# One DMA queue instead of two: bulk loads and gradient stores issued by GpSimd between the zero fill's pieces

## The chip, the cores and the metric

The kernel runs on one core of a Trainium2 chip. The metric is device time in microseconds of that core, the median over several runs. A core has five engines: TensorE (PE, with its weight loads as PEld), VectorE (DVE), ScalarE (ACT), GpSimd (POOL) and SyncE (SP). DMAs that any of them issues are carried out by the core's 16 DMA engines.

## What is computed

One decode step of a transformer block with its whole backward pass. The forward pass is a layer norm, attention of one query token over the last 4,096 positions of a key and value cache, and a gated feed-forward network, with residual sums:

```python
W = min(4096, max(256, Sk // 4))                 # Sk = 32768, so W = 4096
k = repeat(k_cache[:, :, Sk - W:, :], rep)       # B = 2, 8 KV heads, 32 query heads, Dh = 128
v = repeat(v_cache[:, :, Sk - W:, :], rep)
p = softmax(einsum("bhqd,bhkd->bhqk", q, k) * Dh ** -0.5)
h = x + (p @ v).reshape(B, 1, Hq * Dh) @ wo      # D = 512
h2 = h + (gelu(ln(h) @ w_gate) * (ln(h) @ w_up)) @ w_down   # F = 1792
out, vjp = jax.vjp(f, x, k_cache, v_cache, wq, wo, w_gate, w_up, w_down)
return out, *vjp(grad_out)
```

All is bf16. Nine outputs are written: the block's output and eight gradients. Two of them, those of the two caches, have the caches' full size, 2 x 8 x 32768 x 128. Only their last 4,096 positions are not zero, so most of what the kernel writes is zeros: 224 MiB of zeros, 32 MiB of cache gradients that aren't zero, and some 13 MiB of weight gradients.

## The kernel before

**The zero fill.** A tile `zt` of 128 x 2048 bytes is set to zero on POOL (L315). A DMA from it that casts bytes to float32 writes 1 MiB of zeros from all 128 partitions; this is called a column here. There are 32 regions (two caches, two batches, eight heads) of seven columns. `zero_cast(i)` (L110) writes region i with one DMA of seven columns, or, for regions 8, 16 and 24, with six or seven DMAs listed in `ZERO_PARTS` (L107), some of which have 15 rows or fewer, so that the 16 DMA engines do not all receive the same number of bytes. 29 regions are issued at once in `prefetch(0, 0)`; the last three are cut into pieces of one or two columns, and `zero_next` (L127) issues one piece after each store of a cache gradient.

**The stages.** In order: layer norm and query; `attention(0)`, the pass over batch 0's eight KV heads (called groups g); `middle(0)`, the feed-forward network forward and backward with the output projection; `score_grads(0)`, which reads batch 0's V tiles again; the same three for batch 1, the last one interleaved with the weight gradients (`add_group`, L713); the gradient of wq (L801 to L810); and at the end the cache gradients, 16 stores of 2 MiB from eight staging tiles (L823 to L847).

**Memory.** Almost all tiles are byte ranges of one buffer `mem`, at offsets written by hand. Batch 0's K tiles use four slots in turn, so the K of group g+3 can be loaded once group g-1 is done. Batch 0's V tiles have a slot for each group, which batch 1's V tiles take over when `score_grads(0)` has read them. Batch 1's K of groups 5 and 7 take the slot of batch 1's K 0; K 2, 3 and 4 take slots of batch 0's V 5, 6 and 7, and batch 1's V 5, 6 and 7 take them back. `wg` and `wu` share bytes with batch 0's K slots.

**The order of DMAs.** `prefetch(b, g)` (L306) is called at the start of each group and issues that moment's loads: K by `load_k` (L149), V by `load_v` (L153), `wo` (L323), `wg` (L167) and `wu` (L170), all on SP (`nc.sync`). The weight gradients are stored on SP as well (L737, L755, L762, L810). The zeros and the stores of cache gradients are on POOL (`nc.gpsimd`, L114, L130, L844). A scheduler orders PE, DVE and ACT, but SP and POOL are told to keep the order of the program:

```python
ctx.enter_context(tc.manual_schedule(engines={mybir.EngineType.SP, mybir.EngineType.Pool}))
```

So an instruction on SP or POOL that waits for a buffer holds back all that follow it on the same engine.

Of the kernel before, what the change touches and what calls it, by code (L numbers as in the profile page):

```python
# [8 lines left out]
F32 = mybir.dt.float32  # L9
U8 = mybir.dt.uint8  # L10
U32 = mybir.dt.uint32
ACT = mybir.ActivationFunctionType
ALU = mybir.AluOpType
# [3 lines left out]
P = 128  # L17
# [7 lines left out]
F = 1792  # L25
# [43 lines left out]
def kernel(ctx, tc, A_x, A_k_cache, A_v_cache, A_wq, A_wo, B_x, B_w_gate, B_w_up, B_w_down, grad_out,  # L69
# [36 lines left out]

    ZERO_PARTS = {8: ((4, 1), (15, 2), (2, 2), (15, 14), (12, 2), (P, 4), (16, 7)), 16: ((4, 1), (15, 2), (2, 2), (15, 14), (12, 2), (P, 4), (16, 7)), 24: ((3, 16), (15, 2), (3, 4), (15, 18), (12, 2), (P, 4))}  # L107
    ZERO_FIRST, ZERO_CUTS = 29, (1, 1, 1, 2, 2)

    def zero_cast(i):  # L110
        dst, done = zero_regions[i].bitcast(F32), 0
        for rows, n in ZERO_PARTS.get(i, ((P, ZPK // P),)):
            src = zt[0:rows * (P // rows):P // rows, :]
            nc.gpsimd.dma_start(out=dst[done * ZE:(done + rows * n) * ZE].rearrange("(p k e) -> p k e", p=rows, k=n),  # L114
                                in_=src.unsqueeze(1).to_broadcast([rows, n, ZE]))
            done += rows * n
        assert done == ZPK

    zero_pieces = []
    for i in range(ZERO_FIRST, len(zero_regions)):  # L120
        done = 0
        for k in ZERO_CUTS:
            zero_pieces.append(zero_regions[i].bitcast(F32)[done:done + P * k * ZE].rearrange("(p k e) -> p k e", p=P, k=k))
            done += P * k * ZE
        assert done == ZPK * ZE

    def zero_next():  # L127
        if zero_pieces:
            dst = zero_pieces.pop(0)
            nc.gpsimd.dma_start(out=dst, in_=zt[:].unsqueeze(1).to_broadcast([P, dst.shape[1], ZE]))  # L130

# [16 lines left out]

    def load_k(b, g):  # L149
        Kt[b, g] = at(K_OFF[b][g], [P, NJ, DH], BF16, f"K{b}_{g}")  # L150
        nc.sync.dma_start(out=Kt[b, g][:], in_=Kv[:, b, g, :, :])

    def load_v(b, g):  # L153
        Vt[b, g] = at(OFF_V + g * 8 * KIB, [P, NJ, DH], BF16, f"V{b}_{g}")
        nc.sync.dma_start(out=Vt[b, g][:], in_=Vv[:, b, g, :, :])

# [10 lines left out]
    def load_wg():  # L167
        nc.sync.dma_start(out=wg[:], in_=B_w_gate.rearrange("(p r) f -> p r f", r=NDR))

    def load_wu():  # L170
        nc.sync.dma_start(out=wu[:], in_=B_w_up.rearrange("(p r) f -> p r f", r=NDR))

# [133 lines left out]
    def prefetch(b, g):  # L306
        if b == 0:
            if g == 0:
                load_k(0, 0)
                load_wd(OFF_WD0)  # L310
                load_v(0, 0)
                for i in range(1, 4):
                    load_k(0, i)
                    load_v(0, i)
                nc.gpsimd.tensor_scalar(out=zt[:], in0=wq_sb[:, 0, 0:ZE // 2].bitcast(U8),  # L315
                                        scalar1=0, scalar2=None, op0=ALU.mult)
                for i in range(ZERO_FIRST):
                    zero_cast(i)
            elif g + 3 < HKV:
                load_k(0, g + 3)  # L320
                load_v(0, g + 3)
            elif g == 5:
                nc.sync.dma_start(out=wo_sb[:], in_=A_wo.rearrange("(p r) n -> p r n", r=NOR))  # L323
            elif g == 6:
                load_wg()
            elif g == HKV:
                load_wu()
                load_k(1, 0)
                load_k(1, 1)
        else:  # L330
            if g == 0:
                for i in range(5):
                    load_v(1, i)
                for i in range(2, 5):
                    load_k(1, i)
            elif g == 1:
                load_k(1, 5)
            elif g == 2:
                load_k(1, 6)
            elif g < 6:  # L340
                load_v(1, g + 2)
            elif g == 6:
                load_k(1, 7)
            elif g == HKV:
                load_rows(nc.sync)
                load_wd(OFF_WD)
# [351 lines left out]
    with tc.tile_pool(name="ps_G", bufs=2, space=PSUM) as ps_G:  # L698
# [35 lines left out]

        for (r0, nr) in ((0, 14), (14, 14), (28, 4)):
            add_group([D] * nr, lambda k, r0=r0: Ro_flat[:, (r0 + k)::NOR], lambda k: DH_bf[:],
                      lambda st, r0=r0, nr=nr: nc.sync.dma_start(out=gwo_v[:, r0:r0 + nr, :],  # L737
                                                                 in_=st[:, :nr * D].rearrange("p (a n) -> p a n", n=D)))
        row_box = {}

        def rows_from_T(key, srcT_bf):
# [3 lines left out]
            for r in range(NFR):  # L745
                if r == 8:
# [7 lines left out]
        add_group([D] * NFR, lambda k: row_box["act"][:, k::NFR], lambda k: dh2_bf,  # L754
                  lambda st: nc.sync.dma_start(out=gwd_v, in_=st[:, :NFR * D].rearrange("p (a n) -> p a n", n=D)))  # L755
        for (key, srcT, o_dram) in (("dg", dgT_bf, out_6), ("du", duT_bf, out_7)):
            grad_units.append(lambda key=key, srcT=srcT: rows_from_T(key, srcT))
            o_v = o_dram.rearrange("(p r) f -> p r f", r=NDR)
            pieces = [(r, f0, fl) for r in range(NDR) for (f0, fl) in ((0, 512), (512, 512), (1024, 512), (1536, 256))]
            add_group([fl for (_, _, fl) in pieces], lambda k, pieces=pieces: ln2_bf[:, pieces[k][0]::NDR],  # L760
                      lambda k, key=key, pieces=pieces: row_box[key][:, pieces[k][1]:pieces[k][1] + pieces[k][2]],
                      lambda st, o_v=o_v: nc.sync.dma_start(out=o_v, in_=st[:, :NDR * F].rearrange("p (r f) -> p r f", r=NDR)))  # L762
        g_next = [0]
# [9 lines left out]
    with tc.tile_pool(name="ps_W2", bufs=2, space=PSUM) as ps_W, \  # L773
# [27 lines left out]
        for r in range(NDR):  # L801
            st = at(OFF_WQ + r * 8 * KIB, [P, HQ * DH], BF16, "gq")
            for c4 in range(4):
                ps = ps_G.tile([P, 1024], F32, tag="ps_g", name="ps_gq")
                for q in range(2):
                    col0 = c4 * 1024 + q * 512
                    nc.tensor.matmul(out=ps[:, q * 512:(q + 1) * 512], lhsT=L_bf[:, r::NDR],  # L807
                                     rhs=Ro_flat[:, col0:col0 + 512], start=True, stop=True)
                evac(st[:, c4 * 1024:(c4 + 1) * 1024], ps[:])
            nc.sync.dma_start(out=gwq_v[:, r, :], in_=st[:])  # L810

    with tc.tile_pool(name="ps_G3", bufs=3, space=PSUM) as ps_G, \
# [4 lines left out]
        def bd_of(n):  # L817
# [3 lines left out]
            return build_bd(OFF_BD + n * 8 * KIB, rowsb[:], f"bd{n}")  # L821
        nxt = bd_of(0)
        for n, (b, what) in enumerate(jobs):  # L823
            rhs_bd = nxt
            lhs_bf, dst_v = (ds_bf[b], dKv) if what else (p_bf[b], dVv)
            for gq in range(2):
# [15 lines left out]
                for a in range(2):  # L842
                    g0 = gq * 4 + a * 2
                    nc.gpsimd.dma_start(out=dst_v[:, b, g0:g0 + 2, :, :], in_=sts[a][:])  # L844
                    zero_next()
                if gq == 0 and n + 1 < len(jobs):
# [28 lines left out]
```

## Time and profile before

| what | before |
|---|---|
| median of 6 runs | 791.89 us (791.62 to 792.25) |
| the profiled execution | 792.06 us |
| its span | 790.3 us |
| bytes moved by DMA | 332.44 MB, 421 GB/s over the span |
| HBM read, written | 49.30 MB, 282.33 MB |
| busy: PE, DVE, ACT, POOL | 559.3, 473.4, 281.2, 65.6 us |
| POOL's DMAs from `zt` | 61 |
| SP's loads of K and V | 32, of 1 MiB each |

The span runs from the first to the last instruction of the profiled execution; its time is 1.76 us longer. The page cuts the span into 40 slices of 19.76 us; each digit is a busy share in tenths. A queue's line gives packets, MB and the share of the span of 16 engines that its packets took, waiting included. Lines of stretches give start and end, length, the busy time and number of instructions of PE, PEld, DVE, ACT and POOL, then the granted clock of TensorE, the DMA share and GB/s. Lines of waits give who waited for whom, the time in total, how often, and the longest. Lines in order of time give start, duration, engine, line, operation and, in brackets, the idle time before and what ended it.

### The profile page before, as it was taken

To read this page: it belongs to the slowest core of one execution; us is meant where nothing else is said; L and a number is where in the kernel's file an instruction comes from. 1 tells how busy PE (TensorE), PEld (TensorE's weight loads), DVE (VectorE), ACT (ScalarE), POOL (GpSimd) and SP (SyncE) were. 2 spreads that over 40 slices of the span, in tenths; PEclk is the share of its full clock that TensorE was granted. 3 is DMA by queue.
4 is the path that set the end of the run, shared out by engine and by line. 5 is a ranking of instruction groups with operands and counts; after the bars stand their busy time and mean duration, and the time that the engine had idled before them with its cause. 6 is when DMAs were issued, how large, how long until landed. Compare 5 with 4: busy or idle time off the path is not lost. (4 is left out here: it accounts for less than half of the span.)

```text
span 790.3 us, 12404 instructions
## 1 busy us (share of the span) xinstructions
PE 559.3 (71%) x5032; PEld 303.4 (38%) x5096; DVE 473.4 (60%) x1161; ACT 281.2 (36%) x406; POOL 65.6 (8%) x97
## 2 busy tenths in 40 slices
PE   3899998587688988760647877978798766787000
PEld 3656564254566555420423453433233222222000
DVE  2599999126632989770551377675635799898000
ACT  1534330124345424100201352645444466587000
POOL 4300000000020000000030000000000012111100
PEclk9999999868698999895787776975568598799555
DMA  8999999999999999999999999999999999999997
GB/s 366 418 418 422 418 427 424 424 430 428 427 423 418 423 426 423 427 425 428 429 427 429 428 428 427 429 420 427 427 429 427 427 423 427 428 429 426 428 428 291
DMA packets 41418, 332.44 MB, mean 421 GB/s; under 512 B 2432, under 2 KB 2448, under 8 KB 2576
## 3 DMA queue, kind: packets, MB, share of 16 engines
q0 software_dynamic: 34416, 268.44, 88.5%
q1 hardware_dynamic: 6932, 63.19, 37.4%
q8 instruction: 40, 0.66, 0.3%
q10 hardware_dynamic: 12, 0.01, 0.2%
q14 instruction: 18, 0.15, 0.0%
HBM read 49.30 MB, written 282.33 MB: 420 GB/s over the span
## 5 line engine op out<-in xcount | busy, mean ns | idle before, releaser
L422 DVE TENSOR_TENSOR mem<-mem,ee 128x512 bf16<-128x512 bf16 x512 | 181.1, 422 | 42.0 <-PE KT_ps L378 30.6
L433 PE MATMUL M_ps<-mem 128*128 128x512 bf16 x468 | 135.2, 390 | 9.7 <-DVE mem L422 6.1
L836 PE MATMUL ps_g<-mem 128*128 128x512 bf16 x250 | 79.6, 414 | 26.4 <-DVE mem L91 23.8
L380 ACT COPY mem<-KT_ps 128x1024 bf16<-128x1024 bf16 x64 | 63.3, 1014 | 83.8 <-PE KT_ps L378 77.9
L91 DVE CAST mem<-ps_g 128x512 bf16<-128x512 f32 x128 | 82.6, 687 | 9.3 <-ACT mem L93 7.9
L93 ACT CAST mem<-ps_g 128x512 bf16<-128x512 f32 x128 | 74.5, 585 | 33.3 <-PE ps_g L836 26.0
L114 POOL DMA_DIRECT2D out_dram<-zt x46 | 37.0, 1080 | 502.3 <-DMA out_dram<-zt 502.0
L378 PE MATMUL KT_ps<-ident_bf,mem 128*128 128x128 bf16 x512 | 47.1, 237 | 33.7 <-DMA mem<-in_A_k_cache_dram 28.7
L254 PE MATMUL ps_tb<-ident_bf,mem 128*128 128x128 bf16 x480 | 55.8, 250 | 11.4 <-DMA mem<-in_B_w_gate_dram 4.7
L433 PEld LDWEIGHTS <-mem 128*128 128x128 bf16 x512 | 43.6, 99 | 49.1 <-issue 15.2
L836 PEld LDWEIGHTS <-mem 128*128 128x128 bf16 x256 | 26.3, 103 | 79.1 <-issue 66.4
L93 ACT COPY mem<-ps_tb 128x512 bf16<-128x512 bf16 x44 | 25.7, 585 | 74.6 <-PE ps_tb L254 69.8
L254 PEld LDWEIGHTS <-mem 128*128 128x128 bf16 x480 | 37.3, 128 | 36.5 <-issue 30.4
L378 PEld LDWEIGHTS <-mem 128*128 128x128 bf16 x512 | 35.4, 106 | 39.4 <-DMA mem<-in_A_k_cache_dram 29.2
L656 PE MATMUL VT_ps<-ident_bf,mem 128*128 128x128 bf16 x512 | 46.4, 238 | 3.2 <-ACT mem L93 1.1
L656 PEld LDWEIGHTS <-mem 128*128 128x128 bf16 x512 | 36.3, 107 | 27.7 <-issue 20.1
L665 PE MATMUL dP_ps<-mem 128*128 128x512 bf16 x114 | 40.4, 431 | 4.8 <-ACT mem L93 4.7
L93 ACT COPY mem<-VT_ps 128x1024 bf16<-128x1024 bf16 x31 | 31.7, 1022 | 33.5 <-PE VT_ps L656 32.3
L91 DVE COPY mem<-ps_tb 128x512 bf16<-128x512 bf16 x44 | 18.7, 424 | 41.2 <-PE ps_tb L254 39.9
L727 PE MATMUL ps_gr<-mem 2*128 2x512 bf16 (+1 forms) x78 | 33.8, 498 | 12.8 <-DVE mem L747 7.4
L91 DVE CAST mem<-ps_gr 128x512 bf16<-128x512 f32 (+1 forms) x38 | 24.7, 654 | 27.8 <-PE ps_gr L727 27.8
L91 DVE COPY mem<-VT_ps 128x1024 bf16<-128x1024 bf16 x33 | 23.1, 700 | 27.6 <-PE VT_ps L656 27.1
(244 smaller groups left out, 630.5 us busy)
## 6 DMA issues: line engine op xcount, KB each, us to landing
out_dram<-zt POOLq DMA_DIRECT2D x26, 7168.0 KB, 101.8
out_dram<-mem POOLq DMA_DIRECT2D x16, 2048.0 KB, 31.5
mem<-in_A_k_cache_dram SPq DMA_DIRECT2D x16, 1024.0 KB, 22.3
mem<-in_A_v_cache_dram SPq DMA_DIRECT2D x16, 1024.0 KB, 22.7
out_dram<-zt POOLq DMA_DIRECT2D x3, 4096.0 KB, 59.2
out_dram<-zt POOLq DMA_DIRECT2D x6, 2048.0 KB, 32.9
out_dram<-zt POOLq DMA_DIRECT2D x9, 1024.0 KB, 32.9
out_dram<-mem SPq DMA_DIRECT2D x5, 1792.0 KB, 18.9
```

The costliest lines, as they stand in the source:

```text
L91: nc.vector.tensor_copy(out=out, in_=in_)
L93: nc.scalar.copy(out=out, in_=in_)
L114: nc.gpsimd.dma_start(out=dst[done * ZE:(done + rows * n) * ZE].rearrange("(p k e) -> p k e", p=rows, k=n), in_=src.unsqueeze(1).to_broadc ...
L254: nc.tensor.transpose(out=ps[:, a, :], in_=src_block(a), identity=ident_bf[:])
L378: nc.tensor.transpose(out=KT_ps[:, jj, :], in_=Kt[b, g][:, u * 8 + jj, :], identity=ident_bf[:])
L380: nc.scalar.copy(out=KT[:], in_=KT_ps[:])
L422: nc.vector.tensor_tensor(out=pk[:, :, i, :].rearrange("p j (d t) -> p j d t", t=2), in0=Kb[:, j0:j0 + pk_j, :].rearrange("p j (d t) -> p ...
L433: nc.tensor.matmul(out=M_ps[:], lhsT=Vt[b, g][:, j, :], rhs=pk[:, jj, :, :].rearrange("p i d -> p (i d)"), start=(j == 0), stop=(j == NJ - 1))
L656: nc.tensor.transpose(out=VT_ps[:, jj, :], in_=Vt[b, g][:, a * 8 + jj, :], identity=ident_bf[:])
L665: nc.tensor.matmul(out=dP_ps[:, c, :], lhsT=dOpad[:, w0:w0 + P], rhs=VT[:, c * 4:(c + 1) * 4, :].rearrange("d a k -> d (a k)"), start=(i = ...
L727: nc.tensor.matmul(out=ps[:, :n], lhsT=lhsT_fn(k), rhs=rhs_fn(k), start=True, stop=True)
L836: nc.tensor.matmul(out=ps[:, a2, :], lhsT=lhs_bf[:, jp * P:(jp + 1) * P], rhs=rhs_bd[:, ap * 2 + a2, gq * 4:(gq + 1) * 4, :].rearrange("q ...
```

## The change

Four things are done.

1. K, V, `wo`, `wg` and `wu` are loaded on POOL instead of SP, except for the first K and V pairs (groups 0 and 1 of batch 0), and all weight gradients but for small rows are stored on POOL. SP keeps x, wq, w_down, those four tiles and the small rows.
2. The zero fill is no longer issued at once. A function `zeros(n)` issues the next n columns, in DMAs of up to seven; a call with a number written by hand stands behind each load or store.
3. `zt` is made from the first K tile instead of wq.
4. `ZERO_PARTS` holds ten regions instead of three. Regions 5, 15 and 27 have the kind of parts that regions 8, 16 and 24 had; seven others give some rows more to one row's engine.

```diff
-    ZERO_FIRST, ZERO_CUTS = 29, (1, 1, 1, 2, 2)
-    def zero_cast(i): ...
-    def zero_next(): ...
+    ZCOLS = ZPK // P
+    ZERO_PARTS = {5: ((4, 1), (15, 2), (2, 2), (15, 18), (12, 1), (128, 4), (16, 4)), 15: (the same), 27: ((3, 16), (15, 2), (3, 4), (15, 18), (12, 2), (128, 4)),
+                  6: ((6, 2), (1, 6), (9, 2), (12, 2), (4, 1), (128, 6), (16, 4)), ... 7, 14, 16, 17, 18, 19 alike}
+    TAIL_ZEROS = (1, 1, 1, 2, 2, 1, 1, 1, 2, 2, 1, 1, 1, 2, 2, 0)
+    z_cols = [0]
+    def zero_rows(dst, rows, n):
+        src = zt[0:rows * (P // rows):P // rows, :]
+        nc.gpsimd.dma_start(out=dst.rearrange("(p k e) -> p k e", p=rows, k=n),
+                            in_=src.unsqueeze(1).to_broadcast([rows, n, ZE]))
+    def zeros(n):
+        while n:
+            i, c = divmod(z_cols[0], ZCOLS)
+            parts = ZERO_PARTS[i] if c == 0 and n >= ZCOLS and i in ZERO_PARTS else ((P, min(n, ZCOLS - c)),)
+            done = c * P
+            for rows, k in parts:
+                zero_rows(zero_regions[i].bitcast(F32)[done * ZE:(done + rows * k) * ZE], rows, k)
+                done += rows * k
+            z_cols[0] += done // P - c
+            n -= done // P - c
-    def load_k(b, g):        # and load_v alike
+    def load_k(b, g, eng=nc.gpsimd):
-        nc.sync.dma_start(out=Kt[b, g][:], in_=Kv[:, b, g, :, :])
+        eng.dma_start(out=Kt[b, g][:], in_=Kv[:, b, g, :, :])
 # load_wg, load_wu and the load of wo: nc.sync -> nc.gpsimd
     def prefetch(b, g):
         if b == 0:
             if g == 0:
-                load_k(0, 0); load_wd(OFF_WD0); load_v(0, 0); K and V of groups 1 to 3
-                zt from wq; zero_cast(i) for 29 regions
+                load_k(0, 0, nc.sync); load_wd(OFF_WD0); load_v(0, 0, nc.sync); load_k(0, 1, nc.sync); load_v(0, 1, nc.sync)
+                zt from Kt[0, 0]; K and V of groups 2 and 3; zeros(9)
             elif g + 3 < HKV:
                 load_k(0, g + 3)
+                zeros(1)
                 load_v(0, g + 3)
+                zeros(2)
             elif g == 5: load wo;                  +zeros(1)
             elif g == 6: load_wg();                +zeros(7)
             elif g == HKV: load_wu(); load_k(1, 0); load_k(1, 1);   +zeros(27)
         else:
             if g == 0: load_v(1, i), i = 0 to 4;   +zeros(1) behind each
                        load_k(1, i), i = 2 to 4;   +zeros(1), zeros(1), zeros(9)
             elif g == 1: load_k(1, 5);             +zeros(4)
             elif g == 2: load_k(1, 6);             +zeros(5)
             elif g < 6: load_v(1, g + 2);          +zeros((5, 6, 3)[g - 3])
             elif g == 6: load_k(1, 7);             +zeros(62)
 # stores of weight gradients: nc.sync -> nc.gpsimd, with zeros behind each
+ wo's three: 3, 1, 9; w_down: 8; w_gate: 5; w_up: 13; wq's four: 1, 1, 1, 4
 # stores of cache gradients
-                    zero_next()
+                    zeros(tail_zeros.pop(0))
```

## The prediction

> **What bounds the kernel now.** I read the page's slices and queues first.
>
> ```profile
> DMA  8999999999999999999999999999999999999997
> GB/s 366 418 418 422 418 427 424 424 430 428 427 423 418 423 426 423 427 425 428 429 427 429 428 428 427 429 420 427 427 429 427 427 423 427 428 429 426 428 428 291
> ...
> q0 software_dynamic: 34416, 268.44, 88.5%
> q1 hardware_dynamic: 6932, 63.19, 37.4%
> ```
>
> The 16 DMA engines are full in every slice but the first and the last, while PE, DVE and ACT are idle in the last three. DMA is the bound; a faster engine gains nothing. Packets waiting in two queues are counted twice, so the shares sum to over 100%. The change removes no byte, so it can gain only by rate or at the two ends. Next I asked for busy time and GB/s in chosen stretches (last column GB/s):
>
> ```profile
> 0.00:4.00 4.00, 0.26 (x4) 0.18 (x4) 1.75 (x10) 1.58 (x2) 2.73 (x19) 1.00 0.51 141
> ...
> 30.00:60.00 30.00, 29.42 (x401) 18.36 (x406) 26.40 (x83) 11.55 (x15) 0.60 (x1) 1.00 1.15 419
> 164.00:188.00 24.00, 20.52 (x147) 11.20 (x147) 8.15 (x30) 9.00 (x16) 0.53 (x1) 0.83 1.15 429
> ...
> 618.00:636.00 18.00, 13.56 (x38) 4.40 (x38) 14.12 (x20) 10.29 (x17) 0.00 (x0) 0.68 1.13 423
> 660.00:740.00 80.00, 52.04 (x167) 17.20 (x169) 64.92 (x97) 49.89 (x86) 12.50 (x19) 0.86 1.07 427
> ...
> 778.00:784.00 6.00, 0.00 (x0) 0.00 (x0) 0.00 (x0) 0.00 (x0) 0.00 (x0) 0.50 0.87 345
> 784.00:790.00 6.00, 0.00 (x0) 0.00 (x0) 0.00 (x0) 0.00 (x0) 0.00 (x0) 0.50 0.18 76
> ```
>
> Zeros alone (164 to 188) move 429 GB/s. K and V loads on SP beside zeros on POOL: 419. Gradient stores on SP beside zeros: 423, although both only write. From 660 to 740 stores and zeros share POOL's queue: 427. So it is two queues at once that cost about 2%, more than reads against writes. From 778 the engines run dry one after another.
>
> The ledger: 332.44 MB at 429 is 774.9 us; the span is 790.3, so 15.4 us are lost. Start: (429-141)/429 x 4 = 2.7. Twenty-microsecond stretches from 20 to 760 summed in the same way: 6.1, of which 0.5 fall after 640. End: 1.2 + 5.2 = 6.4, of which 2.1 follow the last packet (788.2 in the trace), leaving 4.3 of unevenness. The remainder is rounding.
>
> Last, waits and order in time:
>
> ```profile
> POOL out_dram L114 <- DMA out_dram<-zt: 502.0, 27, 38.7
> ...
> PEld L378 <- DMA mem<-in_A_k_cache_dram: 29.2, 1, 29.2
> ...
> PE ps_tb L254 <- DMA mem<-in_B_w_gate_dram: 4.7, 1, 4.7
> ```
>
> ```profile
> 19.46 7.61 POOL L114 DMA_DIRECT2D out_dram<-zt  x8 [0.31 <-POOL zt L315]
> 58.92 0.60 POOL L114 DMA_DIRECT2D out_dram<-zt  x1 [31.85 <-DMA out_dram<-zt]
> ```
>
> POOL issues eight zero DMAs, then one whenever the eighth before it has landed: at most eight are in flight, here up to 56 MiB. SP does the same (its tenth DMA waits 8.5 us for wq, its second). And the last K load, issued at 346.63, lands 33.8 us later although it is 1 MiB: PE stands for 29 us. That costs nothing now, because zeros go on; it matters once zeros stand behind loads.
>
> **What the Trainium skill says.** "DMA: Bandwidth & Descriptors", Queues, rings and completion order: each engine takes turns between queue rows by whole packets. The late K load agrees: its bytes move from 357 to 364 and its completion comes at 380. Same page, Issuing engines are not separate DMA queues: several issuers save issue time only. This trace agrees and shows a loss besides, 419 against 429. Same page, Latency and other measured facts: some DMA engines lag under software descriptors, by contention that the page calls a guess. No view here names a DMA engine, so I use it for a bound only.
>
> **The change, part by part.** *Issue time.* POOL gains 31 bulk loads and ten gradient stores, and the fill is cut into more pieces; SP loses the 41. POOL's DMA instructions take 0.53 to 0.95 us and the common smallest piece, 1 MiB, takes 2.46 us at 427, so issue stays hidden under transfer; uncovered, 41 x 0.7 = 29 us, hence an upper bound only. The fill has 224 columns of 1 MiB before and after (9+12+1+7+27+16+4+5+14+62+13+8+18+7+21). Its balancing parts change at no byte.
>
> *Start.* SP still brings wq, K, w_down, V, K, V: 9.75 MiB. The zero source now waits for the first K instead of wq, and its 5.37 us operation ends at about 20 to 21 rather than 19.2. SP's loads run to about 27, which hides this: 0 us. Without that cover 2 us.
>
> *One queue.* The 5.6 us lost from 20 to 640 go where two queues overlapped. At the 427.4 of the stretch with one queue, 620 us lose 2.3; stretches of pure zeros lose less, so I take 2.1 and a gain of **3.5**. No row shows loads issued by POOL. At 429, gain 5.5; if loads against zeros keep 419 whatever the queue, 0; if POOL's descriptors for loads make it worse, -3.
>
> *Waits.* Now a POOL wait for a buffer holds back all zeros behind it, and the cover is what is already queued. I lay the bytes in order at 2.46 us per MiB (427), from 2.7 us, and set the drain time against the time SP issued the same load in the trace:
>
> - K for group 4: 22.75 MiB queued, dry at 58.6, issued at 46.2. Margin 12.4. Groups 5, 6, 7: 11.0, 9.9, 9.3.
> - w_gate: 47.75 MiB, 120.1 against 108.3: 11.8. w_up: 141.6 against 130.7: 10.9.
> - Second batch, first V: 87.25 MiB, 217.2 against 214.5: 2.8. Later K 5: 5.4; K 6: 1.7; V 5, 6, 7: 3.1, 4.1, 4.9.
> - K 7: 139.25 MiB, 345.1 against 346.6: -1.5.
>
> But compute moves too. In the old order w_gate lands at 143.2 and PE's transposes of it, placed ahead of the attention product, stall 4.7 us. Queued after 47.75 MiB it lands near 127, so everything after moves 4.7 earlier and the margins become 7.5, 10.1, 6.4, 7.8, 8.8, 9.6 and **+3.2** for K 7. Then K 7 lands about 2 + 2.5 + 2 us after its wait rather than 33.8, and compute gains some 28 us. Its next dependents are the ten gradient stores; their margins in the old times, with w_down's 4.3 us on SP added, are 2 to 9 us (first one 504.4 against 501.7), so with 33 us more they never bind. Central price of waits: 0; bounds 0 and 9. What is late next is nothing but DMA.
>
> *Tail.* 16 stores and 21 zero columns as before, in one queue as before; the staging tiles wait for older stores, which land before 640 by the same count. 0 us.
>
> *End.* Three balanced regions become ten, several giving four extra rows to one engine. In DMA time four 8 KiB rows are four times a per-engine 0.31 us, 1.2 us. The 4.3 us of unevenness can shrink to about 1 (gain 3.3) or, if POOL's larger share makes one engine lag, grow by 3. I take a gain of **1.5**.
>
> Sum: 790.3 - 3.5 - 0 - 1.5 = 785.3 span. The profiled execution took 792.06, 1.76 more than its span, and lies 0.17 above the median of 791.89. So 785.3 + 1.76 - 0.17 = **786.9**.
>
> **Rivals.**
> (a) *POOL's waits empty the DMA engines; slower.* Place: the second batch's K and V waits, K 7 worst. Lateness is paid once, as the largest shortfall, since a pause moves later bytes too. If compute is 10 us later than laid out (the clock row shows PE granted 0.7 to 0.8 at 140 to 220, and w_gate's 4.7 may not come back), K 7 is short by 6.8 plus about 2 to restart: 8.8, giving 786.9 + 8.8 = 795.7. It decides once the shortfall passes 5 us. For it: margins of a few us. Against it: before 140 none is below 9.
> (b) *Nothing moves; same.* The loss is reads against writes and the end keeps its unevenness: 791.9. Against it: 423 with writes alone in two queues, 427 in one.
> (c) *Both gains whole.* 5.5 and 3.3: 790.3 - 8.8 = 781.5, total 783.1.
> (d) *It doesn't do what it says:* SP keeps 10 MB at the start and w_down and rows near 404, so two queues overlap there still. At 2% of 25 us that is 0.5, inside (c)'s and my own range.
>
> **How the numbers follow.** My forecast 0.52, (c) 0.22, (a) 0.18, (b) 0.08. Measurement can tell about 0.2%, or 1.6 us. Faster: 0.52 + 0.22, less small gains, plus a sliver of mild (a): 0.74. Same: 0.08. Slower: 0.18. The range goes from (c) with a margin, 782.0, to the near part of (a), 794.0.
>
> **What would show it.** Right: stretches from 30 to 130 and 236 to 350 at 425 or more; q0 holding over 310 MB; no slice of DMA below 9 between the first and the last; PE's wait for K under 8 us; w_gate's wait gone; the last ten microseconds carrying more than 177 GB/s. Wrong: POOL's waits for DVE or PE ending in a stretch below 400 GB/s near 215, 290 or 345 (then (a)), stretches with loads still at 419 (then (b)), or a longer decay at the end (the balance is off).

## The result, and the profile after

The kernel after the change takes **818.42 us** (median of 10 runs, 815.93 to 821.37), against 791.92 us for the kernel before (20 runs): a ratio of 1.0331, 95% interval [1.0321, 1.0341]. Forecast was 786.9 us, with 782.0 to 794.0 as the range. The change costs 26.5 us instead of gaining 5.

The page's slices and queues of the kernel after, in the same columns as for the kernel before:

```profile
span 815.9 us, 12528 instructions
...
DMA  8999999899999996999999999999999999999996
GB/s 369 410 427 426 422 431 415 306 428 429 423 419 425 421 410 237 427 360 315 426 427 426 427 426 428 427 427 430 429 429 428 427 429 426 429 428 426 429 429 245
...
q0 software_dynamic: 41904, 319.57, 103.0%
q1 hardware_dynamic: 1028, 12.07, 3.8%
```

The change does what it says: q0 carries 320 MB, where before it carried 268. But four slices fall to 360 GB/s or less, where before none between the first and the last was below 418: 306 near 150 us, 237 from 306 to 326, 360 and 315 from 347 to 387. Three more, of 410, 415 and 410, lie a little lower than before. The stretches, in the columns of those shown before (the last is GB/s):

```profile
0.00:4.00 4.00, 0.26 (x4) 0.18 (x4) 1.88 (x10) 1.58 (x2) 2.72 (x19) 1.00 0.49 141
30.00:60.00 30.00, 24.54 (x340) 15.34 (x342) 22.98 (x70) 10.44 (x13) 2.32 (x4) 0.90 1.11 417
60.00:130.00 70.00, 62.55 (x780) 34.81 (x795) 62.42 (x200) 20.38 (x26) 10.25 (x18) 0.97 1.09 425
164.00:188.00 24.00, 19.95 (x193) 13.43 (x193) 6.10 (x26) 6.24 (x11) 3.66 (x6) 0.65 1.15 428
305.00:315.00 10.00, 9.77 (x126) 5.65 (x121) 8.54 (x29) 2.77 (x4) 0.00 (x0) 0.90 0.91 337
315.00:325.00 10.00, 9.52 (x127) 5.20 (x129) 9.69 (x31) 3.17 (x5) 2.00 (x3) 1.00 0.42 126
365.00:375.00 10.00, 9.01 (x84) 4.08 (x84) 10.00 (x31) 0.59 (x1) 5.01 (x8) 1.00 0.41 116
660.00:740.00 80.00, 50.56 (x159) 16.90 (x162) 51.72 (x81) 46.74 (x81) 13.24 (x21) 0.83 1.08 428
```

The start is unchanged (141 GB/s in the first four us). From 315 to 325 PE and DVE are busy for 9.5 of 10 us, while the DMA engines move 126 GB/s. Here compute is the bound, which it was nowhere in the kernel before. Who waits for whom, in total, times and longest:

```profile
POOL out_dram L114 <- DMA out_dram<-zt: 237.2, 40, 15.2
...
POOL mem L148 <- PE M_ps L443: 57.5, 4, 27.1
...
POOL mem L168 <- DVE mem L432: 27.5, 1, 27.5
...
POOL mem L152 <- PE S_ps L398: 23.3, 1, 23.3
```

Before, POOL waited only for zeros to land while it filled (502.0 us), which costs nothing. Now it waits for buffers at the loads of K (L148), V (L152) and `wu` (L168), up to 27.5 us at a time, and every zero stands behind. Three of these waits in POOL's order of time:

```profile
144.55 0.54 POOL L168 DMA_DIRECT2D mem<-in_B_w_up_dram  x1 [27.52 <-DVE mem L432]
```
```profile
318.67 0.55 POOL L152 DMA_DIRECT2D mem<-in_A_v_cache_dram  x1 [23.26 <-PE S_ps L398]
319.20 1.47 POOL L114 DMA_DIRECT2D out_dram<-zt  x2
```
```profile
369.23 0.55 POOL L148 DMA_DIRECT2D mem<-in_A_k_cache_dram  x1 [25.21 <-PE M_ps L443]
369.77 1.89 POOL L114 DMA_DIRECT2D out_dram<-zt  x3
```

Each release falls in one of the stretches that are short of bytes.

**The ledger.** The bytes of the trace's packets, each spread evenly over the packet's time, were summed in steps of 1 us. A step below 395 GB/s counts as part of a hole, and loses (429 - rate)/429 us.

| | before | after |
|---|---|---|
| holes | 0 | 25.9: 141 to 159: 6.2; 284 to 289: 1.0; 312 to 325: 9.2; 363 to 375: 8.5; small ones 1.0 |
| rate lost outside holes, from 20 us to 14 us before the last packet | 6.0 | 3.5 |
| unevenness in the 14 us before the last packet | 4.3 | 5.3 |
| from the last packet to the end of the span | 2.0 | 3.4 |

25.9 - 2.5 + 1.0 + 1.4 = 25.8 us; the spans differ by 815.9 - 790.3 = 25.6. So the holes explain the time. Why compute is late there is the next question.

**The instructions stand in another order.** PE, DVE and ACT are ordered when the program is built, and that order changed although nothing that they do was edited. The table counts, on PE, how many of a group's 32 attention products (`M_ps`) stand ahead of the first and of the last transpose of the next group's K. A negative number means that as many products of the group before are still to come, so that the transposes run far ahead.

```
next group          1        2        3        4        5        6         7
before, batch 0   3, 12    0, 12   -4, 12   -8,  8  -12,  8  -12,  8   -12,  8
after,  batch 0   3, 12    0, 12   -4, 12    0, 12    7, 12   17, 21    21, 25
before, batch 1   0,  0  -24, -8  -40,-12  -40,-12  -40,-12  -40,-12    11, 15
after,  batch 1   0,  0   32, 32    0,  0  -16, -8   29, 32    0,  0    32, 32
```

Where the number is 32, 32, the next group's K is transposed only when all products of the group are issued; its scores and softmax then run in series with the products instead of beside them. DVE's order of time around a maximum of the scores shows it, first before and then after:

```profile
291.66 1.43 DVE L422 TENSOR_TENSOR mem<-mem,ee 128x512 bf16<-128x512 bf16 x4
293.00 0.29 DVE L394 TENSOR_REDUCE mx<-S_ps 128x4 f32<-128x128 f32 x1
293.20 1.09 DVE L422 TENSOR_TENSOR mem<-mem,ee 128x512 bf16<-128x512 bf16 x3
```
```profile
299.31 0.29 DVE L404 TENSOR_REDUCE mx<-S_ps 128x4 f32<-128x128 f32 x1 [5.99 <-PE S_ps L398]
```

Before, the maximum stood amid the multiplications for the group in work. After, DVE had nothing else for 5.99 us. The ends of the groups follow (when ACT takes the result, us):

| | batch 0: fifth to eighth group | batch 1: fourth to seventh group |
|---|---|---|
| before | 100.2, 113.1, 126.0, 137.1 | 316.1, 333.7, 347.7, 392.6 |
| after | 106.6, 119.9, 135.8, 150.5 | 332.2, 344.9, 369.8, 380.8 |

(Before, batch 1's seventh group ends late because the K load of the eighth, whose transposes stand ahead of its last products, landed 33.8 us after its issue, which cost nothing then.)

### The profile page after: what moved, and what is told of

Its sections match the earlier page's. It is cut to its first block, busy times and chain, and to the rows that moved or that the text cites. A ratio compares the mean times of both kernels' runs of the same rounds, so it can differ in the third digit from the quotient of the medians.

```text
span 815.9 us, 12528 instructions
## 1 busy us (share of the span) xinstructions
PE 572.1 (70%) x5036; PEld 305.8 (37%) x5096; DVE 476.0 (58%) x1161; ACT 280.3 (34%) x406; POOL 125.1 (15%) x210
## 4 chain that ended last, share of the span: by engine, by line
PE 33%; DVE 23%; DMA 18%; ACT 8%; issue 4%; POOLq 0%; ACTq 0%; POOL 0%; SPq 0%; DVEq 0%
DMA out_dram<-mem 16%; DVE mem L432 11%; PE M_ps L443 4%; PE ps_tb L251 4%; ACT mem L93 4%; PE VT_ps L666 3%; PE ps_gr L737 3%; PE dP_ps L675 3%; DVE junk L610 3%; ACT mem L390 3%; PE d_ln_ps L595 2%; PE KT_ps L388 2%; PE attn_ps L540 2%; PE gu_ps L552 2%; DMA mem<-in_A_x_dram 2%
## 5 line engine op out<-in xcount | busy, mean ns | idle before, releaser
L432 DVE TENSOR_TENSOR mem<-mem,ee 128x512 bf16<-128x512 bf16 x512 | 177.8, 425 | 6.7 <-PE M_ps L443 6.3
L443 PE MATMUL M_ps<-mem 128*128 128x512 bf16 x472 | 137.8, 396 | 18.0 <-DVE mem L432 13.9
L114 POOL DMA_DIRECT2D out_dram<-zt x133 | 84.0, 664 | 260.1 <-DMA out_dram<-zt 237.2
L852 PE MATMUL ps_g<-mem 128*128 128x512 bf16 x250 | 82.8, 436 | 48.7 <-DVE mem L91 44.4
L443 PEld LDWEIGHTS <-mem 128*128 128x128 bf16 x512 | 45.5, 99 | 62.7 <-issue 25.8
L852 PEld LDWEIGHTS <-mem 128*128 128x128 bf16 x256 | 27.5, 108 | 105.1 <-issue 94.1
L93 ACT COPY mem<-ps_tb 128x512 bf16<-128x512 bf16 x44 | 25.8, 586 | 69.1 <-PE ps_tb L251 64.3
L251 PEld LDWEIGHTS <-mem 128*128 128x128 bf16 x480 | 37.5, 129 | 32.0 <-issue 30.7
L666 PEld LDWEIGHTS <-mem 128*128 128x128 bf16 x512 | 36.2, 106 | 27.2 <-issue 19.8
L388 PE MATMUL KT_ps<-ident_bf,mem 128*128 128x128 bf16 x512 | 45.0, 242 | 1.8 <-DVE mem L683 1.6
L91 DVE CAST mem<-ps_gr 128x512 bf16<-128x512 f32 (+1 forms) x38 | 24.7, 655 | 26.5 <-PE ps_gr L737 26.5
L388 PEld LDWEIGHTS <-mem 128*128 128x128 bf16 x512 | 36.4, 109 | 8.4 <-issue 3.7
L451 ACT CAST mem<-M_ps 128x512 bf16<-128x512 f32 x16 | 9.4, 587 | 87.1 <-PE M_ps L443 87.1
```

Of the source, the lines that this page charges most:

```text
L91: nc.vector.tensor_copy(out=out, in_=in_)
L93: nc.scalar.copy(out=out, in_=in_)
L114: nc.gpsimd.dma_start(out=dst.rearrange("(p k e) -> p k e", p=rows, k=n), in_=src.unsqueeze(1).to_broadcast([rows, n, ZE]))
L251: nc.tensor.transpose(out=ps[:, a, :], in_=src_block(a), identity=ident_bf[:])
L388: nc.tensor.transpose(out=KT_ps[:, jj, :], in_=Kt[b, g][:, u * 8 + jj, :], identity=ident_bf[:])
L432: nc.vector.tensor_tensor(out=pk[:, :, i, :].rearrange("p j (d t) -> p j d t", t=2), in0=Kb[:, j0:j0 + pk_j, :].rearrange("p j (d t) -> p ...
```

## The experiments

**Theory A**: the new queue changes the order of instructions; compute's gates come late, POOL's waits outlast the zeros queued ahead, and the DMA engines run empty. **Rivals**: (B) the order matters little, and the cover of zeros, set too low, would have failed anyway; (C) the loss is a cost of loads in POOL's queue, or of small DMAs, whatever compute does.

### e1_order: K's transposes put back ahead by a constraint

```diff
-                    m_unit(g, u, M_ps)
+                    if u and more:
+                        with tc.issue_after(kt_prev):   # the last transpose of the K unit before
+                            m_unit(g, u, M_ps)
+                    ...
```

> The changed kernel, with an edge that keeps PE from starting the M unit u of a group before the K transposes of the next group that the program puts ahead of it; POOL's queue and all zeros as in the changed kernel. Theory A (the compile-time order of PE's instructions changed, so groups end late, POOL's waits end late and the DMA engines run dry for 25.9 us): most of the emptiness goes; its stretches fall from 25.9 us to 2 to 10 us, span 792 to 800. Theory B (POOL's margins were too thin whatever the order of compute): groups end no earlier, 814 to 818. Theory C (loads queued behind zeros land late and PE waits for them): the new edge makes PE wait for K landings, no better than 816.

Measured: 809.32 us, ratio 1.0222 [1.0195, 1.0249]; holes 15.1 us, the largest 9.5 at 352 to 365. The pairs of 32, 32 and 29, 32 in the table became 4, 12, the first hole fell from 6.2 to 1.4, and 9 us came back. That lies between what theories A and B had led to expect. The constraint does not restore the whole order, so this run doesn't settle how much the order explains.

### e2_cover: the same order, more zeros ahead of the waits

```diff
                 load_wg()
-                zeros(7)
+                zeros(11)
...            K 4 of batch 1: zeros(9) -> 11;  K 6: zeros(5) -> 9;  V 7: zeros(3) -> 7
...            K 7: zeros(62) -> 54;  w_up's stores: zeros(13) -> 7;  uneven regions 14, 15 -> 20, 21
```

> The changed kernel with its compute order, but 14 columns of zeros moved ahead of the waits (4 behind w_gate, 2 behind K 4, 4 behind K 6, 4 behind V 7 of batch 1), taken from the block behind K 7 and from those after w_up's gradient; two balanced regions renumbered so that they still fall in one call. Theories A and B alike: if the lost time is emptiness behind waits, 14 x 2.46 = 34 us of cover more than fills 25.9, the span falls to 815.9 - 25.9 = 790, between 788 and 793, while compute's groups end as late as before. If late compute itself sets the end (a rival), the span stays near 816.

Measured: 800.03 us, 1.0102 [1.0087, 1.0117]; holes 4.3. Page row of this kernel:

```profile
GB/s 366 410 427 424 421 430 426 426 429 427 426 425 426 428 426 429 425 428 428 418 427 427 426 427 421 430 426 429 429 429 425 421 428 363 427 429 426 429 428 177
```

After the first slice none below 410 is left up to 650 us, although the groups still end late (the last at 414.5). So late compute costs nothing by itself; it costs when the queue runs out of zeros. The slice of 363 (2.9 us of hole at 664 to 671) lies in the tail, from which zeros were taken. And the last slice, 177, is worse than after's 245: a loss that the holes seem to have hidden. With the 4.3 us of holes it keeps the span, 797.9 us, above the expected 788 to 793.

### e3_less: less cover at one place

```diff
                 load_wg()
-                zeros(7)
+                zeros(3)
...            load_wu(), K 0, K 1: zeros(27) -> 31
```

> The changed kernel with four columns of zeros moved from in front of w_up's wait to behind the two K loads after it. If emptiness behind a wait costs one to one, the hole near 141 to 159 grows by 4 x 2.46 = 9.8 us and later waits, whose schedule moves with it, lose a part of theirs only if compute doesn't move too: span 822 to 827. If the hole there is hidden by later slack, 816.

Measured: 822.5 us, 1.0384 [1.0367, 1.0402]. Four columns are 4 x 2.46 = 9.8 us of cover; the first hole grew from 6.2 to 16.8 (14.4 at 132 to 149, 2.5 at 152 to 160), by 10.6. All holes together grew by 5.4 only; the four columns stand behind K 1 now and cover something there. The span, 821.0 us, came out just under the expected 822 to 827.

### e4_loads_on_sp: loads back on SP, the rest of the change kept

```diff
-    def load_k(b, g, eng=nc.gpsimd):
+    def load_k(b, g, eng=nc.sync):
...            load_v, w_gate, w_up and wo alike
```

> The changed kernel with K, V, wo, w_gate and w_up loaded on SP again; zeros in the same pieces and order on POOL, gradient stores on POOL. POOL then waits for no buffer before the gradient stores. Theory A and B: no hole before 500; stretches with loads beside zeros fall back to about 420 GB/s; span 788 to 793. The compile-time order of PE is that of the kernel before. If cutting the zeros into pieces or the new balance is what cost time, it stays above 800.

Measured: 797.62 us, 1.0072 [1.0057, 1.0087]; holes 0.3 us. PE's order is that of the kernel before, product by product. So it is the loads' queue that decides the order, and stores, small pieces and parts make no hole. Rate lost: 6.2, as before. Again the end is bad, which puts the span at 796.0 instead of 788 to 793: 9.5 us of unevenness.

### e5_replay: the order of before in the kernel after

```diff
+    ORDER = {"PE": "0+201 202+3 201 ...", "Activation": ..., "DVE": ...}   # before's order of this program's instructions
+    for key, runs in ORDER.items():
+        ...
+        for early, late in zip(want, want[1:]):
+            tc.add_manual_dep(late, early.name, ...)     # order only, no semaphore
```

> The changed kernel, POOL and SP as they are, but PE, DVE and ACT held to the very instruction order of the kernel before by edges between neighbours. Theory A in full (the compile-time order is what made the groups late): groups end at the times of before, the last K lands within 8 us of its wait, emptiness falls from 25.9 us to 0 to 6. With the one slow DMA engine of the cover run (9 us at the end) the span is 790 to 797. Theory B (margins too thin for any order): still over 10 us of emptiness, span over 800.

Measured: 799.4 us, 1.0094 [1.0079, 1.0109]; holes 4.0 instead of 25.9. Nothing but the order of PE, DVE and ACT differs from the kernel after. The page's row of GB/s:

```profile
GB/s 368 410 427 426 416 430 426 413 427 426 423 423 426 429 375 425 426 425 424 429 424 427 426 429 426 428 428 431 427 428 426 428 429 426 428 428 428 427 429 167
```

This is the test of theory A: **the order is worth 22 us of holes**, and 19 us of time, since the end is worse. Rival B is left with the remaining 4.0 us, and C falls: loads and small pieces are all still in POOL's queue. Batch 1's last four groups now end at 331.9, 348.8, 370.2, 381.2: the last is 23 us earlier than in the kernel before, the gain that the forecast had expected from K 7. Batch 0's last four still end 7 to 8 us later than before, at 107.5, 120.7, 133.7 and 144.7. So at least half of their lateness in the kernel after is not the order's. It begins in the second group, where PE stands for 5.1 us (last section), and the zeros queued ahead cover nearly all of it.

### e6_replay_cover and e7_skip: both cures, and more uneven rows

e6 is e5 with e2's zeros. e7 is e6 with two of the seven fine regions (16 and 17; those that give a few rows more to one engine) made as strongly uneven as region 5. A part (15, 18) is one DMA of 15 rows with 18 pieces of 8 KiB each. Where the texts count by how many rows an engine is spared, a row is one such piece; at a sixteenth of 429 GB/s, which is 26.8, it takes one engine 0.31 us.

```diff
# e7
-16: ((10, 2), (1, 6), (5, 2), (12, 2), (4, 1), (128, 6), (16, 4)), 17: ((12, 2), ...)
+16: ((4, 1), (15, 2), (2, 2), (15, 18), (12, 1), (128, 4), (16, 4)), 17: (the same)
```

> Order of before and the 14 columns of cover together: emptiness under 1 us before the tail and none in the tail, since compute there is early again. What is left against before is rate (2 us better) and the end (about 4 us worse): span 791 to 795. If it comes out below 787, the end is better than in the cover run and the one queue pays.

Measured: 799.07 us, 1.0091 [1.0076, 1.0106]. Holes fell to 1.5, but the unevenness at the end rose from e5's 8.8 to 10.5, and almost nothing was gained on e5. Nor is compute early again: the zeros that cover a wait also stand ahead of the next load. K 7 lands 32.7 us after its issue, and PE waits for it as in the kernel before:

```profile
PEld L388 <- DMA mem<-in_A_k_cache_dram: 28.6, 1, 28.6
```

The last group ends at 414.7 (381.2 in e5). That costs no time here, because DMA is the bound again.

> As the run with order and cover, but regions 16 and 17 get the parts of region 5, which leave one DMA engine out of 16 rows each, instead of parts that give four extra rows to another. In the cover run one engine alone (27 GB/s) worked 8 us longer than the rest. If it is the engine that region 5 relieves, 32 rows of 0.31 us or 9.9 us less bring it to the others: span 785 to 788. If it is another engine, the end stays 8 us long or grows: 792 to 798.

Measured: 802.72 us, 1.0137 [1.012, 1.0154]. More uneven rows made the end worse, and the span, 801.3, lies above both expected ranges. With the holes gone, the end is what stands between this kernel and the old one.

### e8_old_balance: e6 with the old kernel's parts

```diff
-5: (..., (15, 18), (12, 1), (128, 4), (16, 4)), 21: (the same), and seven fine regions
+5: (..., (15, 14), (12, 2), (128, 4), (16, 7)), 21: (the same)
```

> As the run with order and cover, but with three balanced regions in the shape that the kernel before has (the relieved engine misses 12, 12 and 16 rows instead of 16, 16 and 16, no region gives extra rows). If the relieved engine is the one that lags, it lags 8 rows or 2.5 us more, span 793 to 798; if the extra rows of the seven regions made the straggler, the end shortens, 787 to 790.

Measured: 793.42 us, 1.002 [1.0012, 1.0029]. The parts cost e6 5.7 us. The span, 791.9, lies between the two expected ranges, so this run alone doesn't tell the causes apart. The last 4 us still run at 26.7 GB/s.

### e9_even and e11_before_even: no uneven parts at all

```diff
-    ZERO_PARTS = {...}
+    ZERO_PARTS = {}        # e9: in e8; e11: in the kernel before
```

> As e8_old_balance (793.42 us, span 791.9, 8.9 us after the last microsecond at full rate), but no region has uneven parts: every DMA of zeros has all 128 partitions, so that each of the 16 engines is dealt the same number of rows. If one engine lags in this queue by itself and the uneven parts relieve it, the straggler at the end grows by most of the 38 rows of relief, 38 x 0.31 = 12 us: about 803. If the uneven parts themselves are what makes an engine late in the one queue, the straggler goes and the run ends when the others do: span 791.9 - 4 = 788, about 789.5. Between the two, about 795, the lag is a part of the relief.

> The kernel before with no uneven parts at all: says what its balance is worth with two queues. If one engine lags by about the relief that the old parts give (38 rows, 12 us), it ends near 791.9 + 10 = 802. If engines are even by themselves, it ends near 791 or at 790, since the 4 us of unevenness at its end go. If e9_even and this one move alike against their balanced twins, the lag belongs to the engine and not to the queue.

Measured: 804.08 us, 1.0153 [1.0138, 1.0169], and 803.58 us, 1.0148 [1.0131, 1.0165]. The end of e9 in stretches:

```profile
770.00:785.00 15.00, 0.00 (x0) 0.00 (x0) 0.00 (x0) 0.00 (x0) 0.00 (x0) 0.50 0.95 383
785.00:799.00 14.00, 0.00 (x0) 0.00 (x0) 0.00 (x0) 0.00 (x0) 0.00 (x0) 0.50 0.07 27
```

A share of 0.07 is one engine of 16, and 27 GB/s is a sixteenth of 429. **One DMA engine is alone for 14 us**, and in e11 for 13, although every DMA of zeros has all 128 partitions. The old parts spare it: e8 and before end 10.7 and 11.7 us sooner.

### e10_no_fine: the strongly uneven new parts alone

```diff
-5, 21, 27 strongly uneven; 6, 7, 16 to 20 fine
+5, 21, 27 strongly uneven
```

> As e6_replay_cover (799.07 us), but the seven regions that give four rows more to one engine are whole again; the three strongly uneven regions keep the sizes of the change (18 rows instead of 14 in the widest part). If the seven regions made the late engine, it comes out like e8_old_balance, 793.4. If the stronger relief in regions 5 and 21 did, it stays at about 799. If relief is what the late engine lacks, it is faster than e8_old_balance by up to 8 rows x 0.31 = 2.5 us, about 791.

Measured: 800.32 us, 1.0106 [1.0091, 1.0121]: the seven fine regions aren't the cause. By their numbers regions 5, 21 and 27 spare one engine 46 rows, more than the old 38. The end:

```profile
782.00:787.00 5.00, 0.00 (x0) 0.00 (x0) 0.00 (x0) 0.00 (x0) 0.00 (x0) 0.50 0.32 133
787.00:796.00 9.00, 0.00 (x0) 0.00 (x0) 0.00 (x0) 0.00 (x0) 0.00 (x0) 0.50 0.07 27
```

The one engine finishes at 795.43, against e9's 799.26: 3.8 us, or 12 rows at 0.307 us (8 KiB at the 26.7 GB/s of the end), and not 46.

### e12_more_relief and e14_before_more_relief: one more region of the old parts

```diff
+19: ((4, 1), (15, 2), (2, 2), (15, 14), (12, 2), (128, 4), (16, 7)),    # e12: in e8; e14: region 12, in the kernel before
```

> As e8_old_balance (793.42 us), with a third region of the old uneven kind (region 19), so that the lagging engine is spared some 11 rows more. e9_even against e8_old_balance gives 10.7 us for the old parts' 36 to 38 rows, 0.29 us a row. If e8_old_balance's last 4 us are still the lagging engine, it ends 11 x 0.29 = 3.2 us earlier: about 790.2, where the other engines end and no more is to be had. If they are an engine that the uneven parts load (12 to 14 rows more than the even ones), nothing is gained: 793.4 or 794.

> The kernel before with a third region of its old uneven kind (region 12). If its last 4 us of unevenness are the lagging engine, as in e11_before_even, it gains up to 11 x 0.29 = 3.2 us: about 788.7. If they are an engine loaded by the uneven parts, 791.7 or somewhat more. Against e12_more_relief it says what one queue is worth when both queues' ends are even.

Measured: **790.46 us**, 0.9982 [0.9975, 0.9989], and **790.05 us**, 0.9978 [0.997, 0.9986]. Both beat both kernels, by 1.4 and 1.8 us on 791.89; e14 was expected at 788.7. The end of e12:

```profile
770.00:781.00 11.00, 0.00 (x0) 0.00 (x0) 0.00 (x0) 0.00 (x0) 0.00 (x0) 0.50 1.08 429
781.00:786.00 5.00, 0.00 (x0) 0.00 (x0) 0.00 (x0) 0.00 (x0) 0.00 (x0) 0.50 0.38 161
```

With equal care for the end, one queue is worth nothing here: 790.46 against 790.05. Batch 1's loads do run faster in it. The same stretch in e14 (two queues) and in e12 (one):

```profile
236.00:345.00 109.00, 94.27 (x1125) 55.55 (x1141) 84.48 (x263) 36.56 (x45) 8.21 (x12) 0.91 1.51 423
```
```profile
236.00:345.00 109.00, 91.98 (x1129) 55.11 (x1147) 77.26 (x239) 37.36 (x45) 14.56 (x23) 0.91 1.12 427
```

Over the run, rate lost is 5.1 us with one queue and 6.1 with two. But from the last packet to the end of the span it takes 3.4 us with one and 2.0 with two.

### e13_split_18, e15_18_without_12x1, e16_14_with_12x1: what the new parts do wrong

```diff
# e13, in e10's regions 5 and 21
-(2, 2), (15, 18), (12, 1)
+(2, 1), (15, 16), (1, 2), (15, 2), (12, 1)
# e15, in the same
-(4, 1), (15, 2), (2, 2), (15, 18), (12, 1), (128, 4), (16, 4)
+(4, 2), (15, 2), (2, 2), (15, 18), (12, 2), (128, 4), (16, 3)
# e16, in e8's regions 5 and 21
-(4, 1), (15, 2), (2, 2), (15, 14), (12, 2), (128, 4), (16, 7)
+(4, 2), (15, 2), (2, 6), (15, 14), (12, 1), (128, 4), (16, 7)
```

> As e10_no_fine (800.32 us), with one thing changed in regions 5 and 21: the DMA of 15 rows with 18 pieces each is issued as 15 rows with 16 pieces, one row with 2, and 15 rows with 2 (the two-row DMA ahead has 1 piece instead of 2). Theory: a DMA with more than 16 pieces to a row is dealt to the engines as 16 and then the rest, so the engine at which the next DMA begins moves by 15, and the later parts spare another engine than the first. By that count e10_no_fine spares the lagging engine 14 rows, e8_old_balance 36 and this kernel 42: 793.4 - 6 x 0.29 = 791.7. Rival: the dealing goes on by rows, whatever the pieces, and this kernel then spares the same engine as e10_no_fine in the first part and is no better: 800 or more.

Measured: 800.92 us, 1.0115 [1.0097, 1.0133]; the one engine finishes at 795.7, as in e10. The theory of 16 and the rest falls. (This kernel also has a hole of 4.3 us at 483 to 492, where POOL waited for the eighth DMA before while several of the eight were small parts.)

> As e10_no_fine (800.32 us), but in regions 5 and 21 the DMA of 12 rows has 2 pieces a row, as in the old parts, instead of 1; the DMA of 15 rows keeps its 18 pieces (4 rows have 2 pieces and 16 rows have 3, to fill the region). Theory H1: a DMA of 12 rows with one piece each does not move on the place at which the next DMA's rows begin, so that all later parts spare other engines; then this kernel spares the lagging engine in all three regions, by 46 rows, and ends like e12_more_relief, 790 to 791. Theory H2: the DMA of 15 rows with 16 or 18 pieces is what shifts it: then nothing changes, about 800.

> The other half: as e8_old_balance (793.42 us), with the DMA of 15 rows at 14 pieces in regions 5 and 21, but the DMA of 12 rows with 1 piece a row, as in the new parts (4 rows with 2 pieces, 2 rows with 6). Theory H1: the lagging engine is spared in the first region alone, about 8 rows, and the time is near 804 - 8 x 0.3 = 801. Theory H2: it is spared in all three, 32 rows, and the time is 793.4 + 6 x 0.3 = 795.

Measured: 791.06 us, 0.999 [0.9981, 0.9999], and 802.55 us, 1.0138 [1.0121, 1.0155]. H1 holds both ways: **the DMA of 12 rows with one piece each is the fault**. Of the parts that differ among e8, e10, e15 and e16, only this one goes with the result: two pieces in e8 and e15, one in e10 and e16. The part of 4 rows has one piece in e8 and e10, and the part of 15 rows has 18 in e10 and e15, a good and a bad end each time. The Trainium skill, "DMA: Bandwidth & Descriptors", Why a DMA increments its semaphore by 16 and not by 1, says that a DMA of fewer than 16 shares from POOL goes to consecutive engines from a cursor that moves on, and that some plain copies are dealt over all 16 by another rule. Counted with such a cursor, the old parts bring it back to the same engine in each region, since the rows of the DMAs below 16 rows sum to 48. If the 12 x 1 copy doesn't move it, the later regions spare others: the count for the first spared engine is then 15 rows in e10 (measured 12), 14 in e13 (12), 8 in e16 (7) and 38 in e8 (35). The cursor itself no run shows, nor which engine is spared.

## Why the prediction was wrong, step by step

- **What bounds the kernel, and what could be gained**: right for the kernel before. That the change removes no byte, so that only rate and ends count, held too.
- **Issue time, 0**: held in the kernel after. POOL's waits for eight zeros back fell from 502 to 237 us, and the large holes end with waits for buffers. e13 shows the limit: small parts among the eight in flight cost 4.3 us.
- **Start, 0**: held to about half a us (slices of 369 and 410 against 366 and 418).
- **One queue, 3.5**: right in sign, too large. At equal ends (e12 and e14) it is 6.1 - 5.1 = 1.0. Loads in batch 1 gained (423 to 427), those at 30 to 60 lost (419 to 417). The 2.5 us seen in the kernel after are not clean, since its engines stood idle in between.
- **Waits, 0 with bounds 0 and 9**: **this is the step that failed**; it cost 25.9. The failing sentence is "I lay the bytes in order at 2.46 us per MiB (427), from 2.7 us, and set the drain time against the time SP issued the same load in the trace". The drain was laid out well: e3's four columns moved the first hole by 10.6 against 9.8. The other side of the comparison, when compute frees the buffer, was copied from a program whose order had been made for other queues. The margins were 3 to 12 us; batch 0's last groups ended 6 to 13 us later, and batch 1's fourth to sixth 11 to 22. With the old order put back (e5), 4.0 of the 25.9 us remain; so the order that a new queue brings is what the step left out. The bound of 9 rested on compute being late by some us for the clock's sake, and a new order was in no bound.
- **w_gate's wait gone, and K 7 landing soon**: both right. PE waits for no K in the kernel after, and K 7 lands within 7.1 us of its issue, by POOL's order of time. The 28 us that compute was to win show up in e5 (23 us) and were used up by the serial order in the kernel after, where the last group ends at 402.7 against 404.3. Of the old late load, only the stretch from 357 to 364, where its bytes go beside zeros, fits turns between the queues. That its first bytes move 10 us after its issue, and its completion comes 16 us after its last, turns by single packets don't explain; it stays open.
- **Tail, 0**: held in the kernel after; e2 shows what it rests on, since zeros taken from it opened 2.9 us.
- **End, a gain of 1.5 with bounds +3.3 and -3**: wrong sign, and outside the bounds once the holes are gone. In the kernel after it cost 1.0 + 1.4. From 315 to 318 us no engine moves a byte, in which time a lagging engine can catch up. That this hides most of the loss fits the runs but has no run of its own: with the new parts and 25.9, 15.1, 4.0 and 1.5 us of holes (after, e1, e5, e6), the unevenness is 5.3, 5.5, 8.8 and 10.5. In e8 with the old parts it is 5.7. The prediction took the 4.3 us of unevenness as rows dealt unequally. In e9 and e11, without uneven parts, it is one engine lagging by 14 and 13 us, most of which the old parts had made up for.
- **Rival (a)** had the mechanism and a chance of 0.18, but two of its terms were too small. "Lateness is paid once" failed: each pause delays the next loads as well, so three places paid 6.2, 9.2 and 8.5. And "before 140 none is below 9" failed for the gate just behind it. **Rival (b)**, nothing moves, is where one queue ends when order, cover and balance are mended: 790.46 against 790.05. The reason is another: the rate gains 1.0 us, and 1.4 more pass after the last packet. **Rival (d)** is out: q0 carried 320 MB.

The signs named as wrong came true: POOL's waits for DVE or PE ending in stretches below 400 GB/s, though near 145, 319 and 369 and not where they were expected. Also, the stretch from 30 to 60 stayed at 417, and the end decayed longer.

## What to carry to other kernels

Moving a load to another queue can reorder the other engines' instructions when a scheduler orders them, so the buffer's release time in the old trace is no longer a fact: compare the instruction orders before setting margins against it, or pin the order. In a queue kept in program order, a wait is safe for as many bytes as stand ahead of it, and these should cover the spread of compute times (here 6 to 22 us later), not their old values. The same bytes also delay the load that they stand ahead of (32.7 us for K 7 in e6), which is free only while nothing but DMA is the bound. Look at the end in steps of one us: a rate of one sixteenth shows that a single engine is still at work, and sparing it 11 rows was worth more here than the queue.

## What the hardware showed unexpectedly

- One of 16 DMA engines lags by 14 us (e9) or 13 (e11) in 800 when no DMA of zeros is uneven. The Trainium skill, "DMA: Bandwidth & Descriptors", Latency and other measured facts, names lagging engines under software descriptors as usual, with a guess at the cause; e9 and e11 agree on the lag, and no view shows the engine's number or the cause.
- Whether each of a part's 12 rows is one piece or two decides how late the end is: 791.06 and 793.42 us with two (e15, e8), 800.32 and 802.55 with one (e10, e16). That later parts then spare other engines is what the count above says; it isn't seen.
- In the kernel after PE stands for 5 us although nothing it waits for shows, and a packet of the instruction queue comes in that time, at 57.6. PE's order of time there:

```profile
54.38 0.59 PE L443 MATMUL M_ps<-mem 128*128 128x512 bf16 x2
60.06 0.38 PE L439 MATMUL oPK_ps<-mem 128*4 128x128 bf16 x8 [5.08 <-issue]
```

The kernel before, e11 and e14 have no such stop. All kernels with the loads on POOL have it, with 4.8 to 5.1 us, and e4 with 2.1. PE goes on 1.3 to 1.6 us after that packet's end in the kernel after, e4, e5 and e12. Instructions fetched late behind zeros would explain it; that wasn't tested.

Left open: why the end of the span follows the last packet 1.4 us later with one queue, and by what estimate the scheduler places K's transposes.
